# Local and global attention with a gated feed-forward: the global queries of four heads on one tile of 128 partitions

## The chip, the core and the metric

The kernel runs on one core of a Trainium2 chip. The metric is the device time of one execution in microseconds. The kernel before takes 1253.52 us (median of three runs, 1249.87 to 1254.31); its profiled execution took 1242.87 us.

## The reference

There are 8 batches of 8 heads, with 512 local and 32 global positions and 64 channels a head. Each global query sees all 544 keys; each local query sees the 32 global keys and the local ones within 32 positions. The result of all heads, 512 wide, goes through a gated feed-forward with 1536 hidden channels.

```
s_g = scale * q_g @ concat(k_g, k_l).T          # 32 x 544 a head
out_g = softmax(s_g) @ concat(v_g, v_l)
s_l = concat(scale * q_l @ k_g.T, where(|i - j| <= 32, scale * q_l @ k_l.T, -1e9))
out_l = softmax(s_l) @ concat(v_g, v_l)
x = attention output as (8 * 544) x 512
y = (sigmoid(x @ w_gate) * (x @ w_val)) @ w_out
```

## The kernel before

**Precision.** The feed-forward, and the attention of most heads, run on TensorE as fp32r with operands split into a high and a low part (`hi`, and `kl` or `lo`), so that two or three products stand for one in fp32. The first heads run natively in fp32 (tiles with `nat` or `first` in their names): batch 0, and the first four heads of batch 1. What is native has no low part to subtract.

**The feed-forward stream** (`ffn_stream`, L380 to L441) sets the order. Per hidden slice of 128 channels and 512 tokens it multiplies twelve matmuls for the gate (`bank_g`), twelve for the value (`bank_v`, both L395) and twelve for the output (`bank_o`, L430), in blocks of four. After each block the generator yields, a clock `now` moves by one unit (half for 256 tokens), and all attention events that have come due are emitted there. A scheduler then orders each engine's instructions within what is emitted. After the opening, the attention of a batch of 512 tokens is emitted during the 108 units of the feed-forward of the batch before. So between the blocks of four feed-forward matmuls stand short visits of attention work.

**Attention events** (`att_events`, L444). A head has two local units of two blocks of 128 queries each and one global unit, four units of `now` apart. A unit is a generator with four stages, run 0, 3, 6 and 9 units after its start (`STAGES`); in the opening the distances are shorter.

**A local unit** (L232): scores for a window of 224 keys a block (L241); mask and maximum on DVE (L255), exp on ACT (L258); scaling by the sum's reciprocal into `p_buf` (L229); four transposes of 128x128 on TensorE (L272), copied by ACT and subtracted by DVE (L283, L284); products with V (L302, L303); copy, sum and sum of halves on ACT, DVE and GpSimd (L305 to L307). Blocks at the two ends of the sequence use masks of their own that blank 32 of the 224 columns.

**A global unit** (`global_unit`, L309) does the same for the 32 global queries of one head on 32 partitions: scores in two PSUM tiles (L321, L323), two maxima on DVE (L326, L327) and their scaling (L328), two exps on ACT (L330, L331), sum, reciprocal and scaling of the 32x576 row tile `pg_buf` on DVE (L333, L334, L229), five transposes of 32 rows (L339), copy and subtraction (L345, L346), and five products with V (L354). For the first two batches V is the stationary operand and the result comes out transposed (L363) into `xg32`; for the others the 32 queries are the rows of the result, collected in `xgq` and transposed at the end (`split_globals`, L531), before the feed-forward of the 256 global tokens.

**Space.** Eight PSUM banks: four for `bank_o`, four in turn for everything else (tag `att`: gate and value accumulators, scores, transposes, products). A bank is free again when its last reader is done. The split V of a head (`vhl`) has two buffers.

**The opening.** Before and beside the first feed-forward items the kernel converts the weights from their 64-bit layout, mostly on DVE (`convert`, L135 to L155).

Of the kernel before, what the change touches and what calls it, by code (L numbers as in the profile page):

```python
# [56 lines left out]
def kernel(ctx, tc, qk, v, w_gate, w_val, w_out, out_l, out_g):  # L57
# [158 lines left out]
    def split_v(T):  # L216
# [14 lines left out]

    def local_unit(T, blocks, x32s, h, col0):  # L232
# [4 lines left out]
        for i, j in enumerate(blocks):  # L237
            qj = ks[0][:, qcol(j) - q0:qcol(j) - q0 + P]
            for t, (kt, k0) in enumerate(zip(ks, k0s)):
                js = slice(k0 + j * BLK, k0 + j * BLK + WIN)  # L240
                nc.tensor.matmul(s_ps[:, i, 0:WIN], qj, kt[:, js], start=t == 0, stop=t == last)  # L241
# [67 lines left out]
    def global_unit(T, b, h):  # L309
        ks, k0s, q0 = T["qk"], T["k0"], T["q0"]  # L310
        nat = T["native"]
        last = len(ks) - 1
# [13 lines left out]
        nc.vector.tensor_reduce(mg[:, 0:1], saf, axis=AX.X, op=ALU.max)  # L326
        nc.vector.tensor_reduce(mg[:, 1:2], sb, axis=AX.X, op=ALU.max)  # L327
        nc.vector.tensor_scalar(mg[:, 2:3], mg[:, 0:1], mg[:, 1:2], -0.125, op0=ALU.max, op1=ALU.mult)  # L328
# [1 line left out]
        nc.scalar.activation(pg[:, 0:512], saf, AF.Exp, bias=mg[:, 2:3], scale=0.125, accum_out=sg[:, 0:1])  # L330
        nc.scalar.activation(pg[:, 544:576], sb, AF.Exp, bias=mg[:, 2:3], scale=0.125, accum_out=sg[:, 1:2])  # L331
        yield
        nc.vector.tensor_scalar(mg[:, 3:4], sg[:, 0:1], sg[:, 1:2], 1e-9, op0=ALU.add, op1=ALU.add)  # L333
        nc.vector.reciprocal(mg[:, 3:4], mg[:, 3:4])  # L334
        scaled(0, pg[:, 0:576], pg[:, 0:576], mg[:, 3:4])
        yield
        pt_ps = ps.tile([P, 5, 32], F32, name="bank_y", tag="att", bufs=4)
        for j in range(5):
            nc.tensor.transpose(pt_ps[:, j], pg[:, j * P:(j + 1) * P], ident[0:32, 0:32])  # L339
        if nat:  # L340
            pt = att.tile([P, 5, 32], F32, name="ptg_nat", tag="ptg", bufs=1)
            nc.scalar.copy(pt, pt_ps)
        else:
            pt = att.tile([P, 5, 64], F32R, name="ptg", bufs=1)
            nc.scalar.copy(pt[:, :, 0:32], pt_ps)  # L345
            nc.vector.tensor_tensor(pt[:, :, 32:64], pt_ps, pt[:, :, 0:32].bitcast(F32), op=ALU.subtract)  # L346
        yield
        vt = T["v"]
        if b > 1:
            g0 = (b - 2) * SG  # L350
            xg = xgq[g0 // P][g0 % P:g0 % P + SG, h * D:(h + 1) * D]
            o_ps = ps.tile([64, 2 * D], F32, name="bank_x", tag="att", bufs=4)
            for j in range(5):
                nc.tensor.matmul(o_ps, pt[:, j, :], vt[:, (VM + VS)[j], :], start=j == 0, stop=j == 4)  # L354
# [253 lines left out]
```

## Time and profile before

| | |
|---|---|
| timed, median of 3 runs | 1253.52 us |
| profiled execution | 1242.87 us |
| its span, first to last instruction | 1240.0 us |
| TensorE busy | 1210.8 us, 98% |
| VectorE (DVE) busy | 884.1 us, 71% |
| ScalarE (ACT) busy | 780.4 us, 63% |
| GpSimd (POOL) busy | 432.4 us, 35% |
| mean granted TensorE clock | 0.989 |

TensorE's busy time counts the overlap of matmuls in flight once, but each matmul's own duration (about 0.4 us for 512 columns) is longer than its distance to the next one. Distances between starts tell what a matmul costs in the stream. A window's row gives its length, the busy time of each engine with the number of instructions, the granted clock, the share of the DMA engines and GB/s. A group's row ends in busy time, mean duration and the idle time just before it, with what ended that.

### The profile page before, as it was taken

What the parts mean: (1) busy time and instruction counts of PE and PEld (TensorE: products, weight loads), DVE (VectorE), ACT (ScalarE), POOL (GpSimd) and SP (SyncE); (2) the same over time, 40 slices, a digit from 0 to 9 for tenths busy, and PEclk for the clock granted to TensorE, in tenths of its full rate; (3) what the DMA queues carried; (4) which work ended last, traced back from release to release, by engine and by line L of the source; (5) the groups of instructions that cost most, each with busy time, mean ns of one, the idle gap of its engine ahead of it and who ended that gap; (6) DMA issues with size and microseconds to landing.
All of it is one profiled execution on the core that took longest, in us unless ns stands there. A gap on an engine that the chain in (4) does not pass through costs nothing.

```text
span 1240.0 us, 20451 instructions
## 1 busy us (share of the span) xinstructions
PE 1210.8 (98%) x6892; PEld 990.1 (80%) x6892; DVE 884.1 (71%) x2555; ACT 780.4 (63%) x1901; POOL 432.4 (35%) x453
## 2 busy tenths in 40 slices
PE   8899989999999999999999999999999999999998
PEld 6677768887887888888888888887787888888897
DVE  6798976868777777867776877777876777633343
ACT  5677767756666676757765776766675677523233
POOL 2334443524444244434443444424443444100000
PEclk9799989999999999999999999999999999999999
DMA  6677854333333333333333343333333332121243
GB/s 227 216 246 237 271 183 119 105 111 109 91 104 112 121 93 110 110 109 102 112 97 117 118 110 109 93 115 109 98 105 123 102 92 89 51 100 54 69 136 119
DMA packets 59495, 151.88 MB, mean 122 GB/s; under 512 B 6144, under 2 KB 19456, under 8 KB 59392
## 3 DMA queue, kind: packets, MB, share of 16 engines
q1 hardware_dynamic: 59392, 150.59, 39.8%
q8 instruction: 54, 0.88, 0.3%
q14 instruction: 49, 0.40, 0.1%
HBM read 135.36 MB, written 15.20 MB: 121 GB/s over the span
## 4 chain that ended last, share of the span: by engine, by line
PE 82%; DVE 11%; ACT 3%; issue 2%; DMA 1%; POOL 0%; DVEq 0%; ACTq 0%; POOLq 0%
PE bank_v L395 21%; PE bank_g L395 21%; PE bank_o L430 19%; PE bank_x L241 5%; PE bank_y L272 4%; PE bank_y L339 2%; PE bank_x L321 2%; PE bank_x L303 2%; PE bank_x L302 2%; DVE p_buf L229 2%; DVE bank_v L414 1%; DVE bank_v L413 1%; PE bank_x L354 1%; DMA out_dram<-ob 1%; ACT s_sb L258 1%
## 5 line engine op out<-in xcount | busy, mean ns | idle before, releaser
L395 PE MATMUL bank_g<-xt,wg 128*128 128x512 f32 (+1 forms) x1440 | 339.4, 371 | 3.2 <-DVE hh L417 1.5
L430 PE MATMUL bank_o<-wo,hh 128*128 128x512 f32 x1224 | 333.1, 403 | 0.6 <-ACT hh L416 0.3
L395 PE MATMUL bank_v<-xt,wv 128*128 128x512 f32 (+1 forms) x1440 | 332.2, 368 | 0.9 <-DVE mn L408 0.3
L395 PEld LDWEIGHTS bank_g<-xt,wg 128*128 128x128 f32 x1440 | 238.7, 191 | 43.4 <-DVE hh L417 3.8
L395 PEld LDWEIGHTS bank_v<-xt,wv 128*128 128x128 f32 x1440 | 237.6, 190 | 38.9 <-issue 1.3
L430 PEld LDWEIGHTS bank_o<-wo,hh 128*128 128x128 f32 x1224 | 215.4, 189 | 39.5 <-ACT hh L416 2.3
L258 ACT ACTIVATE s_sb<-s_sb,nm 128x224 f32<-128x224 f32 x240 | 113.9, 475 | 103.1 <-DVE nm L255 101.9
L210 POOL TENSOR_TENSOR kl<-qk_raw,qk_hi 128x704 fp32r<-128x704 f32 x52 | 88.6, 1704 | 192.9 <-ACT qk_hi L209 192.9
L229 DVE TENSOR_SCALAR p_buf<-s_sb,r 128x128 f32<-128x128 f32 (+1 forms) x443 | 132.5, 344 | 4.3 <-PE bank_y L272 0.7
L307 POOL TENSOR_TENSOR x<-t 64x256 f32<-64x256 f32 x104 | 78.1, 751 | 150.6 <-DVE t L306 146.7
L403 ACT ACTIVATE th<-bank_g 128x512 f32<-128x512 f32 (+1 forms) x120 | 63.4, 529 | 101.0 <-PE bank_g L395 100.3
L408 DVE TENSOR_SCALAR mn<-bank_g 128x512 f32<-128x512 f32 (+1 forms) x108 | 67.1, 622 | 78.7 <-ACT th L403 77.2
L416 ACT CAST hh<-bank_v 128x512 fp32r<-128x512 f32 (+1 forms) x120 | 62.6, 522 | 86.4 <-DVE bank_v L414 85.6
L413 DVE TENSOR_TENSOR bank_v<-bank_v,mn 128x512 f32<-128x512 f32 (+1 forms) x120 | 73.5, 612 | 46.1 <-PE bank_v L395 37.3
L255 DVE CUSTOM_DVE_ANT_0 s_sb<-bank_x,masks 128x224 f32<-128x224 f32 x240 | 84.3, 383 | 27.9 <-PE bank_x L241 25.8
L272 PE MATMUL bank_y<-ident,p_buf 128*128 128x128 f32 x496 | 78.4, 279 | 9.3 <-DVE p_buf L229 6.9
L209 ACT CAST qk_hi<-qk_raw 128x1248 fp32r<-128x1248 f32 x52 | 64.2, 1234 | 33.0 <-PE bank_y L323 31.8
L272 PEld LDWEIGHTS bank_y<-ident,p_buf 128*128 128x128 f32 x496 | 58.6, 141 | 32.9 <-DVE t L306 8.3
L417 DVE TENSOR_TENSOR hh<-bank_v,hh 128x512 fp32r<-128x512 f32 (+1 forms) x120 | 72.1, 601 | 17.3 <-ACT hh L416 16.8
L212 POOL TENSOR_TENSOR qk_hi<-qk_raw,qk_hi 64x256 fp32r<-64x256 f32 x104 | 81.5, 804 | 4.1
L306 DVE TENSOR_TENSOR t<-bank_x,t 64x512 f32<-64x512 f32 x104 | 70.4, 677 | 10.8 <-ACT t L305 10.3
L284 DVE TENSOR_TENSOR pt<-bank_y,pt 128x512 fp32r<-128x512 f32 x104 | 70.5, 678 | 9.8 <-ACT pt L283 9.7
(120 smaller groups left out, 1925.3 us busy)
## 6 DMA issues: line engine op xcount, KB each, us to landing
wo<-wo_dram SPq DMA_DIRECT2D x116, 512.0 KB, 3.4
qk_raw<-in_qk_dram SPq DMA_DIRECT2D x104, 312.0 KB, 4.4
v_raw<-in_v_dram SPq DMA_DIRECT2D x52, 256.0 KB, 2.6
out_dram<-ob SPq DMA_DIRECT2D x34, 256.0 KB, 2.7
xt<-in_w_gate_dram SPq DMA_DIRECT2D x12, 512.0 KB, 4.6
xt<-in_w_val_dram SPq DMA_DIRECT2D x12, 512.0 KB, 4.0
xt<-in_w_out_dram SPq DMA_DIRECT2D x12, 512.0 KB, 4.4
v_nat<-in_v_dram SPq DMA_DIRECT2D x8, 512.0 KB, 5.2
```

The source lines that it names most:

```text
L210: nc.gpsimd.tensor_tensor(kl, t[:, K0:Q1], hi[:, K0:Q1].bitcast(F32), op=ALU.subtract)
L212: nc.gpsimd.tensor_tensor(hi[64:128, r], t[64:128, r], hi[64:128, r].bitcast(F32), op=ALU.subtract)
L229: nc.vector.tensor_scalar(out, in_, by, None, op0=ALU.mult)
L255: anchor[0] = nc.vector.tensor_tensor_reduce(out=s_sb[:, i], in0=s_ps[:, i, 0:WIN], in1=masks[:, m], scale=-0.125, scalar=3.0e38, op0=ALU. ...
L258: nc.scalar.activation(s_sb[:, i], s_sb[:, i], AF.Exp, bias=nm[:, i:i + 1], scale=-1.0, accum_out=sm[:, i:i + 1])
L272: nc.tensor.transpose(pt_ps[:, 2 * i + t], pb[:, i, t * P:(t + 1) * P], ident)
L284: nc.vector.tensor_tensor(pt[:, 1], pt_ps, pt[:, 0].bitcast(F32), op=ALU.subtract)
L307: nc.gpsimd.tensor_tensor(dst, t0[:, :, 0], t0[:, :, 1], op=ALU.add)
L395: nc.tensor.matmul(acc, w[a][:, t, fs], xt[:, c, t, x0:x0 + ntok], start=n == 0, stop=n == 11)
L413: nc.vector.tensor_tensor(acc, acc, mn, op=ALU.mult)
L417: nc.vector.tensor_tensor(hh[:, 1, 0:ntok], acc, hh[:, 0, 0:ntok].bitcast(F32), op=ALU.subtract)
L430: nc.tensor.matmul(o_ps[t], ph[:, a, t * P:(t + 1) * P], pwo[:, c], start=f2 == 0 and i == 0, stop=f2 == NF - 1 and i == 2)
```

## The change

The global queries of four heads (`GH = 4`) share one tile. `global_unit` becomes two functions. `global_scores` runs for each head at its old place: it multiplies the scores and lets ACT copy them, unscaled, to the head's 32 partitions of `pg`, which now has 128. `global_group` runs once every four heads, right after the fourth head's scores: one maximum, one exp, one scaling for all 128 rows, in one stage; six units later five transposes of 128x128 into two PSUM banks, copy and subtraction; three units later 20 products with V (5 for each head) into one bank, and one copy, one sum and one sum of halves. It always writes the queries as rows to `xgq`, which now has two tiles of 128; `xg32` is gone. For native heads the probabilities become the stationary operand and V the moving one (64 elements in place of 32). V's buffers go from two to five.

Beside that, the first and last blocks of a sequence compute only their 192 columns that count (`span`): scores, maximum, exp and one scaling are narrower, two of the three masks go, and the host's layout of the side tiles of V shifts by 32 rows to fit.

The diff, cut to its core:

```diff
+KALL = SL + SG
+GH = 4
 STAGES = (0, 3, 6, 9)
+GSTAGES = (0, 6, 9)
...
-    pg = const.tile([32, 5 * P], F32, name="pg_buf")
+    pg = const.tile([P, 5 * P], F32, name="pg_buf")
...
-        vhl = spl.tile([P, 8, 2 * D], F32R, name="vhl")
+        vhl = spl.tile([P, 8, 2 * D], F32R, name="vhl", bufs=GH + 1)
...
+    def span(j):
+        return (32 if j == 0 else 0), (WIN - 32 if j == 3 else WIN)
...
+            w0, w1 = span(j)
             for t, (kt, k0) in enumerate(zip(ks, k0s)):
-                js = slice(k0 + j * BLK, k0 + j * BLK + WIN)
-                nc.tensor.matmul(s_ps[:, i, 0:WIN], qj, kt[:, js], start=t == 0, stop=t == last)
+                js = slice(k0 + j * BLK + w0, k0 + j * BLK + w1)
+                nc.tensor.matmul(s_ps[:, i, w0:w1], qj, kt[:, js], start=t == 0, stop=t == last)
...
-    def global_unit(T, b, h):
+    def global_scores(T, row):
...
-        mg = small.tile([32, 4], F32, name="mg")
-        saf = sa.rearrange("p a c -> p (a c)")
-        nc.vector.tensor_reduce(mg[:, 0:1], saf, axis=AX.X, op=ALU.max)
-        nc.vector.tensor_reduce(mg[:, 1:2], sb, axis=AX.X, op=ALU.max)
...
+        rows = slice(SG * row, SG * (row + 1))
+        nc.scalar.copy(pg[rows, 0:SL], sa.rearrange("p a c -> p (a c)"))
+        nc.scalar.copy(pg[rows, SL:KALL], sb)
+
+    def global_group(Ts, b, g):
+        nat = Ts[0]["native"]
+        mg = small.tile([P, 4], F32, name="mg")
+        p = pg[:, 0:KALL]
+        nc.vector.tensor_reduce(mg[:, 0:1], p, axis=AX.X, op=ALU.max)
+        nc.vector.tensor_scalar(mg[:, 1:2], mg[:, 0:1], -0.125, None, op0=ALU.mult)
+        nc.scalar.activation(p, p, AF.Exp, bias=mg[:, 1:2], scale=0.125, accum_out=mg[:, 2:3])
+        nc.vector.tensor_scalar_add(mg[:, 3:4], mg[:, 2:3], 1e-9)
+        nc.vector.reciprocal(mg[:, 3:4], mg[:, 3:4])
+        scaled(0, p, p, mg[:, 3:4])
         yield
+        banks = [ps.tile([P, n, GH, SG], F32, name="bank_y", tag="att", bufs=4) for n in (4, 1)]
+        for j in range(5):
+            o = banks[j // 4][:, j % 4].rearrange("p r q -> p (r q)")
+            nc.tensor.transpose(o, pg[:, j * P:(j + 1) * P], ident)
...
+        o_ps = ps.tile([2 * SG, GH, 2 * D], F32, name="bank_x", tag="att", bufs=4)
+        for r, T in enumerate(Ts):
+            for j in range(5):
+                nc.tensor.matmul(o_ps[:, r], pt[:, j, r].rearrange("p c q -> p (c q)"), T["v"][:, tiles[j], :],
+                                 start=j == 0, stop=j == 4)
+        y = att.tile([SG, GH, 2 * D], F32, name="yq", tag="t0", bufs=1)
...
+                if i == nu:
+                    ev.append((t0, 2, lambda T=T, h=h: global_scores(T, h % GH)))
+                    if h % GH < GH - 1:
+                        continue
+                for o in STAGES if i < nu else GSTAGES:
```

On TensorE, in a steady batch, this is a stretch of the program before (one head's five transposes, L339, and its five products, L354, between feed-forward blocks L395 and L430 and a local unit's scores L241):

```order
L395 MATMUL bank_g<-xt,wg_113 128x512 x4
L339 MATMUL bank_y<-ident,pg_buf 128x32 x5
L395 MATMUL bank_v<-xt,wv_115 128x512 x4
L395 MATMUL bank_v<-xt,wv_116 128x512 x4
L241 MATMUL bank_x<-qk_hi 128x224
L241 MATMUL bank_x<-kl,qk_hi 128x224
L241 MATMUL bank_x<-qk_hi 128x224
L241 MATMUL bank_x<-kl,qk_hi 128x224
L395 MATMUL bank_v<-xt,wv_115 128x512 x4
L354 MATMUL bank_x<-vhl,ptg 64x128 x5
```

Such a pair of visits stands there for every head. In the changed program the stretch behind a fourth head's scores is this (L389 and L424 are the feed-forward, L300 and L301 a local unit's products with V, L339 the group's transposes; after them eight more L424 and then `L360 MATMUL bank_x<-vhl,ptg 64x128 x20`, the group's products):

```order
L389 MATMUL bank_v<-xt,wv_110 128x512 x4
L389 MATMUL bank_v<-xt,wv_111 128x512 x4
L300 MATMUL bank_x<-pt,vhl 128x256
L301 MATMUL bank_x<-pt,vhl 128x256
L300 MATMUL bank_x<-pt,vhl 128x256
L301 MATMUL bank_x<-pt,vhl 128x256
L389 MATMUL bank_v<-xt,wv_110 128x512 x4
L339 MATMUL bank_y<-ident,pg_buf 128x128 x5
L424 MATMUL bank_o_3135<-wo,hh 128x512
L424 MATMUL bank_o_3136<-wo,hh 128x512
L424 MATMUL bank_o_3137<-wo,hh 128x512
L424 MATMUL bank_o_3138<-wo,hh 128x512
```

The five transposes are now as wide as a local unit's, and heads one to three of a group leave only their scores in the row. On DVE, before, one head's softmax (L326 to L229 on `pg_buf`) stands like this ahead of a local unit's sum of products (L306) and subtraction (L284):

```order
L326 TENSOR_REDUCE mg<-bank_x 32x1
L327 TENSOR_REDUCE mg<-bank_y 32x1
L328 TENSOR_SCALAR mg<-mg 32x1
L333 TENSOR_SCALAR mg<-sg 32x1
L334 RECIPROCAL mg<-mg 32x1
L229 TENSOR_SCALAR pg_buf<-pg_buf,mg 32x576
L306 TENSOR_TENSOR t_6335<-bank_x,t_6335 64x512
L284 TENSOR_TENSOR pt<-bank_y,pt 128x512
```

In the changed program DVE has the group's softmax (L329 to L222 on `pg_buf`) and, later, its two subtractions (L345) among the feed-forward's operations (L402 to L411):

```order
L329 TENSOR_REDUCE mg<-pg_buf 128x1
L330 TENSOR_SCALAR mg<-mg 128x1
L332 TENSOR_SCALAR mg<-mg 128x1
L333 RECIPROCAL mg<-mg 128x1
L222 TENSOR_SCALAR pg_buf<-pg_buf,mg 128x544
L304 TENSOR_TENSOR t_4339<-bank_x,t_4339 64x512
L282 TENSOR_TENSOR pt<-bank_y,pt 128x512
L402 TENSOR_SCALAR mn<-bank_g 128x512
L304 TENSOR_TENSOR t_4385<-bank_x,t_4385 64x512
L407 TENSOR_TENSOR bank_v<-bank_v,mn 128x512
L345 TENSOR_TENSOR ptg<-bank_y,ptg 128x16x32
```

The block of softmax operations stands in DVE's row once for four heads; the operation that waits for exp (L332) has the same local operations behind it as L333 before.

More of the change, by code (lines that the diff above doesn't have):

```diff
@@ L193, in load_v @@
             if T["h"] % ng == 0:
-                t = spl.tile([P, ng, nw, D], F32, name="v_nat", tag="vhl")
+                t = spl.tile([P, ng, nw, D], F32, name="v_nat", tag="vhl", bufs=GH + 1)
                 nc.sync.dma_start(t, v[n:n + ng, :, c].rearrange("n p j d -> p n j d"))
@@ new lines, in global_group @@
+    def global_group(Ts, b, g):
[8 more added lines that the diff above has]
+        scaled(0, p, p, mg[:, 3:4])
+        yield
+        banks = [ps.tile([P, n, GH, SG], F32, name="bank_y", tag="att", bufs=4) for n in (4, 1)]
+        for j in range(5):
+            o = banks[j // 4][:, j % 4].rearrange("p r q -> p (r q)")
+            nc.tensor.transpose(o, pg[:, j * P:(j + 1) * P], ident)
+        pt = att.tile([P, 5, GH, 2, SG], F32 if nat else F32R, name="ptg_nat" if nat else "ptg", tag="ptg", bufs=1)
+        for bank, t in zip(banks, (pt[:, 0:4], pt[:, 4:5])):
+            hi, lo = t[:, :, :, 0], t[:, :, :, 1]
+            nc.scalar.copy(hi, bank)
+            if not nat:
+                nc.vector.tensor_tensor(lo, bank, hi.bitcast(F32), op=ALU.subtract)
@@ L336, in global_unit @@
         yield
-        pt_ps = ps.tile([P, 5, 32], F32, name="bank_y", tag="att", bufs=4)
-        for j in range(5):
-            nc.tensor.transpose(pt_ps[:, j], pg[:, j * P:(j + 1) * P], ident[0:32, 0:32])
+        g0 = b * SG
+        xg = xgq[g0 // P][g0 % P:g0 % P + SG, g * GH * D:(g + 1) * GH * D].rearrange("q (r d) -> q r d", d=D)
+        tiles = VM + VS[:1]
         if nat:
[L341 to L354, printed above, removed]
-            y = att.tile([32, 2 * D], F32, name="yq", bufs=1)
-            nc.scalar.copy(y, o_ps[32:64])
-            nc.vector.tensor_tensor(y, o_ps[0:32], y, op=ALU.add)
-            nc.gpsimd.tensor_tensor(xg, y[:, 0:D], y[:, D:], op=ALU.add)
-            return
@@ L360, in global_unit @@
-        xg = xg32[prow:prow + 64, kt, b * SG:(b + 1) * SG]
-        o_ps = ps.tile([64, 32] if nat else [P, 64], F32, name="bank_x", tag="att", bufs=4)
-        for j in range(5):
-            nc.tensor.matmul(o_ps, vt[:, (VM + VS)[j], :], pt[:, j, :], start=j == 0, stop=j == 4)
-        if nat:
+            o_ps = ps.tile([SG, GH, D], F32, name="bank_x", tag="att", bufs=4)
+            for r, T in enumerate(Ts):
+                for j in range(5):
+                    nc.tensor.matmul(o_ps[:, r], pt[:, j, r, 0], T["v"][:, tiles[j], :], start=j == 0, stop=j == 4)
@@ L531, in split_globals @@
     def split_globals():
[L532 to L534 removed]
+        g0 = 0
         for q in xgq:
```

65 lines of the change are left out of this document (25 added, 40 removed).

## The prediction

> **What bounds the kernel now.** I read the page's busy table first, then the windows by stage, then TensorE's timeline inside one batch, then the groups by form and the waits.
>
> ```profile
> span 1240.0 us, 20451 instructions
> PE 1210.8 (98%) x6892; PEld 990.1 (80%) x6892; DVE 884.1 (71%) x2555; ACT 780.4 (63%) x1901; POOL 432.4 (35%) x453
> 56.00:168.50 112.50, 101.94 (x681) 79.99 (x681) 103.60 (x269) 82.25 (x245) 47.05 (x34) 0.97 0.77 249
> 531.00:667.00 136.00, 135.88 (x758) 110.81 (x757) 101.81 (x307) 91.88 (x214) 56.22 (x60) 1.00 0.37 109
> ...
> L152 DVE SCALAR_TENSOR_TENSOR xt<-xt 128x512 uint32<-128x512 uint32 x27 | 24.6, 911 | 0.0
> ```
>
> TensorE is busy 98% of the span. The two windows (columns after the length: PE, PEld, DVE, ACT, POOL busy, granted clock) show two stages. A steady batch, 531 to 667, holds TensorE without a gap; DVE has a quarter of the time free and ACT a third. Six such batches fill 260 to 1075. In the opening, 56 to 168.5, DVE is busy 103.6 of 112.5 us (92%) most of all with converting weights (its costliest group in this window is L152's, the last row), and TensorE stands idle 112.5 - 101.9 = 10.6 us. So in the batches only what TensorE's own stream sheds counts; in the opening DVE work counts too.
>
> Matmul busy times overlap, so I price a visit of attention work between feed-forward matmuls by start times. TensorE's timeline of one head:
>
> ```profile
> 676.32 2.93 PE L430 MATMUL bank_o<-wo,hh 128*128 128x512 f32 x12
> 679.09 1.09 PE L395 MATMUL bank_g<-xt,wg 128*128 128x512 f32 x4
> ...
> 682.33 1.10 PE L395 MATMUL bank_v<-xt,wv 128*128 128x512 f32 x4
> 683.26 0.60 PE L272 MATMUL bank_y<-ident,p_buf 128*128 128x128 f32 x4
> 683.62 2.11 PE L395 MATMUL bank_v<-xt,wv 128*128 128x512 f32 x8
> 685.56 0.28 PE L321 MATMUL bank_x<-qk_hi 128*32 128x256 f32 x1
> ...
> 692.88 1.09 PE L395 MATMUL bank_g<-xt,wg 128*128 128x512 f32 x4
> 693.90 0.49 PE L339 MATMUL bank_y<-ident,pg_buf 32*128 32x32 f32 x5
> 694.32 2.13 PE L395 MATMUL bank_v<-xt,wv 128*128 128x512 f32 x8
> 696.29 0.27 PE L241 MATMUL bank_x<-qk_hi 128*128 128x224 f32 x1
> 696.40 0.27 PE L241 MATMUL bank_x<-kl,qk_hi 128*128 128x224 f32 x1
> ...
> 696.73 1.11 PE L395 MATMUL bank_v<-xt,wv 128*128 128x512 f32 x4
> 697.68 0.46 PE L354 MATMUL bank_x<-vhl,ptg 128*64 128x128 f32 x5
> 697.98 1.13 PE L430 MATMUL bank_o<-wo,hh 128*128 128x512 f32 x4
> 698.95 0.60 PE L272 MATMUL bank_y<-ident,p_buf 128*128 128x128 f32 x4
> ```
>
> Twelve feed-forward matmuls take 679.09 - 676.32 = 2.77 us, 0.231 each. From 692.88 to 696.29 there are twelve of them and the five global transposes: 3.41 - 2.77 = **0.64 us** for the visit. From 682.33 to 685.56, twelve and four full 128x128 transposes: 3.23 - 2.77 = 0.46, or 0.115 each. From 696.73 to 698.95, eight and the five global products with V: 2.22 - 1.85 = **0.37**; within it they follow each other at 0.30 / 5 = 0.06, so 0.07 is the price of the visit itself.
>
> **The change part by part.** *Global transposes.* Five per group of four heads replace twenty. They now have the shape of the local ones, so 5 x 0.115 = 0.58 us. A batch has eight heads, two groups: 8 x 0.64 - 2 x 0.58 = 3.96 us less.
>
> [...]
>
> *Products with V.* Twenty in one visit, same shape: 20 x 0.06 + 0.07 = 1.27 us in place of 4 x 0.37 = 1.48; two groups, 0.42 us less. Six batches: 6 x (3.96 + 0.42) = **26.3 us**.
>
> The other 16 heads stand in the opening: batch 0, native fp32, and batch 1, whose first four heads are native too. Their four groups: the group of split heads saves 4 x 0.64 - 0.58 + 0.42 / 2 = 2.2 us. The three native groups save 3 x (4 x 0.64 - 0.58) = 5.9 on transposes. Their products with V swap operands:
>
> ```profile
> 57.76 1.05 PE L321 MATMUL bank_x<-qk_nat 64*32 64x256 f32 x4
> 58.65 0.22 PE L323 MATMUL bank_y<-qk_nat 64*32 64x32 f32 x2
> ...
> 59.47 0.77 PE L363 MATMUL bank_x<-ptg_nat,v_nat 128*64 128x32 f32 x10
> 60.16 0.74 PE L395 MATMUL bank_v<-xt,wv 128*128 128x256 f32 x4
> ```
>
> Before, ten instructions (two per fp32 product) take 0.69 us a head, 0.069 each. After, 64 elements move instead of 32. A 256-element native one takes 0.89 / 4 = 0.22, so 64 take 0.055 if time goes by length: between 0.055 and 0.11 (twice 0.055) each, -1.7 to +4.9 us over the 120 instructions. I take 0, nearest to the row 0.069. **8.1 us** in all for this stage's TensorE work.
>
> *Softmax.* These are the DVE and ACT operations of one global head now:
>
> ```profile
> L326 DVE TENSOR_REDUCE mg<-bank_x 32x1 f32<-32x512 f32 x64 | 43.1, 673 | 10.9 <-PE bank_y L323 8.2 <-PE bank_x L321 2.6
> L327 DVE TENSOR_REDUCE mg<-bank_y 32x1 f32<-32x32 f32 x64 | 10.9, 170 | 0.0
> L328 DVE TENSOR_SCALAR mg<-mg 32x1 f32<-32x1 f32 x64 | 12.8, 200 | 1.9
> L333 DVE TENSOR_SCALAR mg<-sg 32x1 f32<-32x1 f32 x64 | 12.8, 200 | 48.6 <-ACT pg_buf L331 47.5
> L334 DVE RECIPROCAL mg<-mg 32x1 f32<-32x1 f32 x64 | 9.5, 149 | 1.4
> L229 DVE TENSOR_SCALAR pg_buf<-pg_buf,mg 32x576 f32<-32x576 f32 x64 | 46.1, 720 | 1.5
> L330 ACT ACTIVATE pg_buf<-bank_x,mg 32x512 f32<-32x512 f32 x64 | 43.1, 673 | 10.7 <-DVE mg L328 10.5
> L331 ACT ACTIVATE pg_buf<-bank_y,mg 32x32 f32<-32x32 f32 x64 | 16.8, 262 | 0.0
> L305 ACT COPY t<-bank_x 64x512 f32<-64x512 f32 x104 | 60.6, 583 | 12.3 <-PE bank_x L303 10.3
> ```
>
> On DVE a head costs 0.673 + 0.170 + 0.200 + 0.200 + 0.149 + 0.720 = 2.11 us; a 512-wide operation takes 0.673 on 32 partitions (L326) and 0.678 on 128 (L284, below), so a whole group costs about 0.72 + 0.2 + 0.2 + 0.15 + 0.68 = 1.95 where four heads cost 8.4. ACT gets two copies a head, 0.583 + 0.26, and one exp a group where it had two exps a head, so it is lighter too. In the batches TensorE's stream hides all this: DVE had 34 us free in 136. In the opening it does not. About nine heads lie in 56 to 168.5; 9 x 2.11 = 19 us of DVE become about 4. DVE's load falls from 103.6 to some 88 in 112.5, and the 10.6 us that TensorE waits there, plus the clock that it loses after them, can shrink. Bounds: 0, if the waits are chains and not load, and 10.6. I take **6 us**, nearer to the upper row, since the waits I can see are for DVE:
>
> ```profile
> 113.67 0.47 PE L339 MATMUL bank_y<-ident,pg_buf 32*128 32x32 f32 x5 [1.94 <-DVE pg_buf L229]
> ...
> 168.52 0.63 PE L272 MATMUL bank_y<-ident,p_buf 128*128 128x128 f32 x4 [3.63 <-DVE p_buf L229]
> ```
>
> *The chain of a group.* Copies 0.583 + 0.262, maximum 0.72, scale 0.2, exp about 0.71, sum and reciprocal 0.35, scaling 0.68: 3.5 us without queues. On TensorE, between the fourth head's scores and the group's transposes, stand 24 feed-forward matmuls and three local visits: 24 x 0.231 + 0.46 for transposes + 2 x 0.46 for products (four matmuls of half the width each, so four halves of 0.231) = 6.9 us. The margin of 3.4 us covers ACT's and DVE's queues. Behind the transposes stand twelve matmuls, 2.8 us, and in them the ACT copies and DVE subtractions of two banks:
>
> ```profile
> L345 ACT CAST ptg<-bank_y 128x160 fp32r<-128x160 f32 x52 | 15.1, 291 | 11.3 <-PE bank_y L339 10.8
> L284 DVE TENSOR_TENSOR pt<-bank_y,pt 128x512 fp32r<-128x512 f32 x104 | 70.5, 678 | 9.8 <-ACT pt L283 9.7
> DVE mg L333 <- ACT pg_buf L331: 47.5, 38, 1.8
> PEld bank_y L272 <- DVE t L306: 8.3, 18, 0.6
> ```
>
> A 512-wide copy is 0.58, the subtraction 0.68 and the small one about 0.3: 1.6 us against 2.8, where one head's 160-wide pair had cost 0.6 (L345 0.29 and as much on DVE). Feed-forward work on DVE stands in between (0.68 each), so the twenty products may wait: 0 to 0.7 us (one such operation), I take 0.2 for 12 groups in the batches, **-2.4 us**. In DVE's row the maximum, the wait for exp and the scaling stand in one block, and behind it the local unit's addition that frees a bank. That is not new: DVE waited 38 times for exp, 1.25 us each, now 16 times at most.
>
> *Edges.* The first and last blocks multiply 192 columns, not 224. A 224-column matmul follows the one before at 0.11 us (696.29 to 696.40); by length 192 take 0.016 less, over 208 of them 3.3 us; at a fixed price 0. Four 128-column transposes also took 0.115 apart, so I take the fixed price nearly whole: **0.5 us**. Shorter exps and maxima lie on DVE and ACT under cover. The mask copies and memsets at the start stand beside the first loads: nothing. The last global tile of 128 rows in place of 64, and four small splits less, stand under 2.8 us of feed-forward matmuls as before: nothing; about 0.3 us if not.
>
> **Sum.** 26.3 + 8.1 + 6 - 2.4 + 0.5 = 38.5 us. Against the profiled execution of 1242.87 us (span 1240.0 and 2.87 around it) that is 1204.4. The three timed runs have a median of 1253.52, 10.65 above the profiled one; I take the same microseconds off it: **1215 us**.
>
> **The rivals.**
>
> *A, the opening gives nothing.* DVE's remaining conversions keep TensorE waiting as long, and waits at 20 products rise to 0.7 us for 12 groups. The windows speak for it (92% of DVE, most of it weights). Then 26.3 + 8.1 + 0.5 - 8.4 = 26.5: 1227 us.
>
> *B, the banks.* Attention and feed-forward share four PSUM banks. A group's transposes take two at once for copy and subtraction, and the products a third for 0.58 + 0.68. If the feed-forward accumulators wait for them, every group loses the 1.6 us above: 16 x 1.6 = 26 us, and 1241 us remains. For it: L272 waited 18 times for the addition that frees a bank. Against: each wait was under 0.6, and the heads hold their score banks for a copy instead of a maximum and an exp.
>
> *C, slower: the group comes late.* If the chain, with what is queued on ACT and DVE, is longer than its 6.9 us (less in the opening, where mostly half-width matmuls stand between), TensorE idles at the transposes, and then the clock drops:
>
> ```profile
> 114.90:118.20 3.30, 3.30 (x19) 3.24 (x19) 2.09 (x5) 1.49 (x3) 1.76 (x1) 0.50 0.61 136
> ```
>
> After the idle 1.94 us before 113.67 the granted clock is 0.50 for 3.3 us, which costs another 1.7. A group that is 2 us late would lose 3.7, sixteen of them 59: 1215 + 59 = 1274 us. It ends slower from 38.5 / 16 = 2.4 us per group on, that is a delay of about 0.7 us and the dropped clock, each time. Against: in the batches the margin is 3.4 us, and the granted clock of 531 to 667 is 1.00.
>
> [...]
>
> *D, it saves nothing on TensorE:* the transposes' time was other work's shadow. The start times exclude it in the batches.
>
> **How the numbers follow.** Forecast 0.70, A 0.17, B 0.06, C 0.06, D 0.01. The range: below, all 10.6 us of the opening, the 1.7 us of the swapped products, the 3.3 us of full edge price and no waits at the products make 38.5 + 4.6 + 1.7 + 2.8 + 2.4 = 50.0 us, 1203.5, rounded to 1203. Above, A with the swapped products at 4.9 us dearer, 1232, and a little of B: 1236. B still ends over 0.5% faster (the three runs spread 4.4 us, 0.35%; 0.5% is about what can be told from no change). Faster 0.92, same 0.03, slower 0.05.
>
> **What would show it.** In the profile after: 80 group transposes at about 0.58 us a visit and 20 products at 1.27; a steady batch 4.3 us shorter, about 131.2 us; DVE under 0.9 of its time in 56 to 168 and fewer idle microseconds of TensorE there. Wrong if TensorE waits at the group's transposes or products for DVE in the batches, if the accumulators wait for ptg's subtraction, or if half-clock windows follow the group visits.

## The result and the profile after

The changed kernel takes 1262.68 us (median of four runs, 1260.87 to 1263.75) against 1253.61 for the kernel before in the same runs: a ratio of 1.0077, 95% interval 1.0053 to 1.0101. The prediction was 1215 us, so it had the wrong sign. The profiled execution of the kernel before was faster than its timed runs here (1242.87 us, not 1253.61), so between the two profiles the loss is larger, 19.1 us of span (1240.0 to 1259.1).

The profiled execution took 1260.87 us. Its page begins like this, and the window row below it is a steady batch, a section of 432 feed-forward matmuls (length, then PE, PEld, DVE, ACT, POOL busy, granted clock, DMA share, GB/s):

```profile
span 1259.1 us, 19319 instructions
...
PE 1182.2 (94%) x6652; PEld 986.0 (78%) x6652; DVE 782.3 (62%) x2186; ACT 754.8 (60%) x1719; POOL 414.9 (33%) x408
...
509.90:652.50 142.60, 133.29 (x723) 110.98 (x722) 88.87 (x259) 88.84 (x193) 54.48 (x54) 0.98 0.36 103
```

TensorE has 240 instructions less and 28.6 us less busy time than before (1210.8). Yet its idle time, span minus busy, is 1259.1 - 1182.2 = 76.9 us; before it was 29.2. DVE and ACT are both lighter. So the saving is there and something new makes TensorE wait, in the steady batches: this one takes 142.6 us and not 135.6. The same section of the kernel before:

```profile
515.70:651.30 135.60, 135.49 (x753) 110.46 (x752) 101.45 (x307) 91.91 (x215) 56.23 (x60) 1.00 0.37 109
```

The changed kernel's waits say for what (engine, tile and line, what it waited for: total us, times, longest):

```profile
PE bank_y L319 <- DMA out_dram<-ob: 22.9, 4, 6.2
PE bank_y L319 <- DVE mn L402: 6.3, 2, 6.0
PE bank_v L389 <- DVE pt L282: 9.7, 12, 2.7
PE bank_x L300 <- DVE pt L282: 9.1, 8, 1.7
ACT vhl L214 <- DMA v_raw<-in_v_dram: 84.8, 36, 4.1
POOL vhl L215 <- ACT vhl L214: 103.3, 43, 3.7
SPq L193 <- POOL vhl L215: 121.5, 48, 7.0
SPq L193 <- DMA v_raw<-in_v_dram: 77.8, 31, 5.2
```

None of TensorE's large waits is at the group's transposes or products. The new row is ACT's: 84.8 us at L214, the cast of a head's V into its high part, waiting for the load of that V. Before, the same cast had none; its group's row in that kernel ends in the idle time ahead of it:

```profile
L221 ACT CAST vhl<-v_raw 128x512 fp32r<-128x512 f32 x52 | 31.9, 614 | 0.0
```

Five times, once in a batch, TensorE stands some 6 us at L319, the small score matmul. One of those places on TensorE, DVE, ACT and SP (start, duration, what, and in brackets the idle time ahead with its releaser):

```profile
686.66 0.28 PE L317 MATMUL bank_x<-kl,qk_hi 128*32 128x256 f32 x1
692.49 0.23 PE L319 MATMUL bank_y<-qk_hi 128*32 128x32 f32 x1 [5.54 <-DMA out_dram<-ob]
...
689.92 0.69 DVE L432 TENSOR_SCALAR ob<-bank_o 128x512 f32<-128x512 f32 x1 [5.46 <-DMA out_dram<-ob]
...
691.74 0.69 DVE L402 TENSOR_SCALAR mn<-bank_g 128x512 f32<-128x512 f32 x1 [0.85 <-ACT th L397]
...
679.72 0.62 ACT L214 CAST vhl<-v_raw 128x512 fp32r<-128x512 f32 x1 [1.97 <-DMA v_raw<-in_v_dram]
680.25 0.58 ACT L410 CAST hh<-bank_v 128x512 fp32r<-128x512 f32 x1
...
684.29 0.62 ACT L214 CAST vhl<-v_raw 128x512 fp32r<-128x512 f32 x1 [2.55 <-DMA v_raw<-in_v_dram]
...
672.54 14.10 SPq L193 DMA_DIRECT2D v_raw<-in_v_dram  x4
686.73 0.86 SPq L433 DMA_DIRECT2D out_dram<-ob  x2
```

Read it from the bottom. SP's queue has four V loads in a row. V as loaded has one buffer, so each load waits until the head before has been cast (0.62 us) and subtracted (1.29 us, the median on GpSimd): the last two casts start 4.57 us apart, and the four loads hold the queue for 14.10 us. Two output stores stand behind them and go out at 686.73. Until they land, DVE's copy into `ob` (L432) waits, and L402, the last reader of a gate accumulator, stands behind it on DVE; TensorE's L319 needs that bank. Meanwhile ACT has stood 1.97 and 2.55 us at casts with feed-forward work queued behind.

The two windows of that place show what follows:

```profile
686.70:692.50 5.80, 0.26 (x4) 0.01 (x1) 1.69 (x5) 1.84 (x4) 0.00 (x0) 0.94 0.88 281
692.50:698.00 5.50, 5.50 (x19) 4.62 (x20) 3.90 (x9) 3.71 (x7) 2.80 (x3) 0.50 0.11 40
```

After 5.8 us with hardly any matmul the granted clock is 0.50 for 5.5 us more.

Where do the bunches come from? ACT's row in the scheduled order has three casts of V in nine rows, where before one stands every twenty or so:

```
L214 CAST vhl<-v_raw 128x8x64
L397 ACTIVATE th<-bank_g 128x512
L404 ACTIVATE th<-th 128x512
L403 ACTIVATE mn<-mn 128x512
L214 CAST vhl<-v_raw 128x8x64
L410 CAST hh<-bank_v 128x512
L255 ACTIVATE s_sb,sm<-s_sb,nm 128x192
L255 ACTIVATE s_sb,sm<-s_sb,nm 128x224
L214 CAST vhl<-v_raw 128x8x64
```

With V for a cast of V and Q for one of queries and keys, a batch reads `VVVVQQQQVVQVVQQQ` now and `QVQVQVQVQVQVQVQV` before.

### The profile page after: what moved, and what is told of

It is laid out like the page before. It is cut to its first block, busy times and chain, and to the rows that moved or that the text cites. A ratio compares the mean times of both kernels' runs of the same rounds, so it can differ in the third digit from the quotient of the medians.

```text
span 1259.1 us, 19319 instructions
## 1 busy us (share of the span) xinstructions
PE 1182.2 (94%) x6652; PEld 986.0 (78%) x6652; DVE 782.3 (62%) x2186; ACT 754.8 (60%) x1719; POOL 414.9 (33%) x408
## 4 chain that ended last, share of the span: by engine, by line
PE 66%; DVE 11%; ACT 8%; DMA 7%; POOL 4%; issue 4%; SPq 0%; POOLq 0%; DVEq 0%; ACTq 0%
PE bank_o L424 18%; PE bank_v L389 17%; PE bank_g L389 16%; DMA v_raw<-in_v_dram 5%; PE bank_x L238 4%; PE bank_y L270 3%; POOL vhl L215 3%; ACT s_sb L255 3%; DMA out_dram<-ob 2%; DVE p_buf L222 2%; PE bank_x L300 2%; PE bank_x L301 2%; PE bank_x L317 1%; DVE xt L144 1%; DVE s_sb L252 1%
## 5 line engine op out<-in xcount | busy, mean ns | idle before, releaser
L389 PE MATMUL bank_v<-xt,wv 128*128 128x512 f32 (+1 forms) x1440 | 332.5, 368 | 9.7 <-DVE pt L282 9.7
L424 PE MATMUL bank_o<-wo,hh 128*128 128x512 f32 x1224 | 337.6, 408 | 3.0 <-DVE hh L411 2.0
L389 PE MATMUL bank_g<-xt,wg 128*128 128x512 f32 (+1 forms) x1440 | 333.8, 367 | 0.9 <-POOL xt L372 0.5
L389 PEld LDWEIGHTS bank_v<-xt,wv 128*128 128x128 f32 x1440 | 240.6, 192 | 46.6 <-issue 9.3
L389 PEld LDWEIGHTS bank_g<-xt,wg 128*128 128x128 f32 x1440 | 239.1, 191 | 38.7 <-issue 2.1
L424 PEld LDWEIGHTS bank_o<-wo,hh 128*128 128x128 f32 x1224 | 222.6, 194 | 44.5 <-DVE hh L411 2.8
L255 ACT ACTIVATE s_sb<-s_sb,nm 128x192 f32<-128x192 f32 (+1 forms) x240 | 110.6, 462 | 91.8 <-DVE nm L252 91.5
L222 DVE TENSOR_SCALAR p_buf<-s_sb,r 128x128 f32<-128x128 f32 (+2 forms) x443 | 116.7, 301 | 8.0 <-PE bank_y L270 2.4
L402 DVE TENSOR_SCALAR mn<-bank_g 128x512 f32<-128x512 f32 (+1 forms) x108 | 67.5, 625 | 84.1 <-ACT th L397 83.2
L411 DVE TENSOR_TENSOR hh<-bank_v,hh 128x512 fp32r<-128x512 f32 (+1 forms) x120 | 72.9, 608 | 60.7 <-ACT hh L410 60.7
L252 DVE CUSTOM_DVE_ANT_0 s_sb<-bank_x,masks 128x192 f32<-128x192 f32 (+1 forms) x240 | 80.6, 369 | 34.4 <-PE bank_x L238 25.8
L215 POOL TENSOR_TENSOR vhl<-v_raw,vhl 128x512 fp32r<-128x512 f32 x52 | 67.3, 1294 | 104.0 <-ACT vhl L214 103.3
L270 PEld LDWEIGHTS bank_y<-ident,p_buf 128*128 128x128 f32 x496 | 62.5, 144 | 28.8 <-DVE p_buf L222 6.7
L214 ACT CAST vhl<-v_raw 128x512 fp32r<-128x512 f32 x52 | 32.1, 618 | 87.1 <-DMA v_raw<-in_v_dram 84.8
```

The costliest lines, as they stand in the source:

```text
L215: nc.gpsimd.tensor_tensor(vhl[:, :, D:2 * D], t, vhl[:, :, 0:D].bitcast(F32), op=ALU.subtract)
L222: nc.vector.tensor_scalar(out, in_, by, None, op0=ALU.mult)
L252: anchor[0] = nc.vector.tensor_tensor_reduce(out=s_sb[:, i, w], in0=s_ps[:, i, w], in1=mid[:, w], scale=-0.125, scalar=3.0e38, op0=ALU.add ...
L255: nc.scalar.activation(s_sb[:, i, w], s_sb[:, i, w], AF.Exp, bias=nm[:, i:i + 1], scale=-1.0, accum_out=sm[:, i:i + 1])
L270: nc.tensor.transpose(pt_ps[:, 2 * i + t], pb[:, i, t * P:(t + 1) * P], ident)
L389: nc.tensor.matmul(acc, w[a][:, t, fs], xt[:, c, t, x0:x0 + ntok], start=n == 0, stop=n == 11)
```

## The experiments

Each run is compared with runs of the kernel before on the same chip (medians of these 1243.2 us for the first four kernels, 1250.6 for the next four, 1242.2 for the four after and 1249.8 for the last), so its ratio counts more than its microseconds. Theories of the first four runs: **Q** (queue): the 20 products release V of four heads at once, the schedule then puts V's loads and casts in bunches, and engines and queues stand at them. **N**: the number of V buffers alone does it. **G**: the group's own visits, banks and DVE block cost the time.

### Buffers alone, paced loads, paced casts, stores elsewhere

*`before_v5`*, the kernel before with V's buffers at five:

```diff
-        vhl = spl.tile([P, 8, 2 * D], F32R, name="vhl")
+        vhl = spl.tile([P, 8, 2 * D], F32R, name="vhl", bufs=5)
```

> The kernel before with one edit: V's split buffers go from two to five, as in the change. Theory Q (queue): the stalls come from V's buffers that fall free four at a time after the twenty products, so that V loads stand in bunches on the DMA queue; five buffers that fall free one at a time do nothing, ratio to before 0.995 to 1.005. Rival N (number): the five buffers alone let the scheduler place V casts and loads too early, ratio 1.01 to 1.03. Rival G (group): the group's own visits, banks and DVE block cost the time; nothing here, 0.995 to 1.005.

Measured: 1244.23 us, ratio to the kernel before 1.0009 (0.9964 to 1.0055). N is out; the order still has one V load a head.

*`load_paced`*, the changed kernel with each V load queued on SP behind the last output-weight load or output store (`sp_last`):

```diff
-        nc.sync.dma_start(t[:, c], v[n][:, c])
+        with tc.issue_after(sp_last[0].ins):
+            nc.sync.dma_start(t[:, c], v[n][:, c])
```

> The changed kernel with each V load queued behind the last wo load or output store that the program emitted before it, so no V load stands ahead of an older store. Theory Q: the waits of about 6 us at the small score product (L319), once a batch, go with the half clock after them, 6 x (5.7 + 1.7) = 44 us; about 1218 us, 1212 to 1232. Rival G: the waits stay, 1255 to 1265. Rival N: partly, 1240 to 1255, since ACT still has its casts ahead of the loads.

Measured: 1229.54 us, ratio 0.9874 (0.9806 to 0.9942), inside Q's range. The 6 us waits at L319 are gone, but not all of the loss (lines are two higher here):

```profile
PE bank_g L391 <- DVE pt L284: 20.1, 10, 4.5
...
ACT vhl L216 <- DMA v_raw<-in_v_dram: 43.9, 15, 5.9
```

ACT still stands 43.9 us at casts, and TensorE waits 20.1 us for the subtraction that follows ACT's copy of `pt`. The edit moves the casts too: ACT's row reads `QVQVQVQVQVQVQQVV` a batch here, so this run alone doesn't tell SP's queue from ACT's.

*`cast_paced`*, the changed kernel with each V cast queued on ACT behind the last emitted exp of a local unit (`act_last`):

```diff
-        nc.scalar.copy(vhl[:, :, 0:D], t)
+        with tc.issue_after(act_last[0].ins):
+            nc.scalar.copy(vhl[:, :, 0:D], t)
```

> The changed kernel with each V cast on ACT queued behind the last local exp that the program emitted before it. Theory Q: ACT no longer waits for V loads (84.8 us before this edit, under 10 after), the single raw V buffer is released late and evenly, so the loads spread out as well; both the 6 us waits and the 1.7 us waits of local products go: about 1215 us, 1208 to 1228. Rival G: 1255 to 1265.

Measured: **1202.51 us, ratio 0.966 (0.9596 to 0.9723)**. The order has one V load and one cast a head again. The page, a steady batch, the cast's group row (busy, mean ns | idle ahead) and TensorE's largest waits:

```profile
PE 1162.4 (97%) x6652; PEld 974.6 (81%) x6652; DVE 809.8 (67%) x2186; ACT 753.3 (63%) x1719; POOL 415.6 (35%) x408
...
493.90:626.40 132.50, 130.51 (x724) 109.73 (x723) 93.06 (x259) 88.80 (x193) 54.76 (x54) 1.00 0.39 111
...
L216 ACT CAST vhl<-v_raw 128x512 fp32r<-128x512 f32 x52 | 31.5, 606 | 0.0
...
PE bank_v L391 <- DVE pt L284: 11.8, 12, 1.0
PE bank_x L302 <- DVE pt L284: 4.8, 6, 1.3
```

The cast waits for nothing. The same 6652 TensorE instructions take 19.8 us less busy time than in the changed kernel (mean granted clock 0.991 in place of 0.975), and idle falls from 76.9 to 1201.9 - 1162.4 = 39.5 us. So the grouped queries do bring about what they should. The last two rows, 16.6 us, are the large new ones among TensorE's waits (the kernel before has 0.2 us at that subtraction); they are what is left for G.

*`store_act`*, the changed kernel with the output stores on ACT's queue:

```diff
-                            nc.sync.dma_start(C2["dst"][t * P:(t + 1) * P, :], ob)
+                            nc.scalar.dma_start(C2["dst"][t * P:(t + 1) * P, :], ob)
```

> The changed kernel with the output stores issued from ACT's queue in place of SP's; V loads stay in bunches. Theory Q: the stores no longer stand behind V loads, the 6 us waits go, the 1.7 us waits of local products for ACT (17 us in all) stay: about 1225 us, 1218 to 1238. Rival G: 1255 to 1265. If the bunched loads hurt by other ways than the stores (wo loads behind them), also 1245 to 1260.

Measured: 1258.35 us, ratio 1.0097 (1.0061 to 1.0133), far above Q's 1218 to 1238. The 6 us wait splits in two, of up to 2.9 us at L317 and 2.3 at L319, and ACT's wait at casts stays (86.9 us, 36 times). This doesn't tell SP from ACT, since ACT's own stores stand behind its blocked casts: two go out at 684.64, right behind the cast at 683.50 that had waited 2.53 us.

### Is it holding V, or the group?

**O** is Q made sharper: V freed in fours leads the schedule to place casts in ACT's row ahead of loads that have not landed.

*`before_hold`*, the kernel before with five V buffers and, at each fourth head, four one-element products that keep all four in use till then:

```diff
+        held.append(vt)
+        if h % 4 == 3:
+            for i, u in enumerate(held):
+                nc.vector.tensor_tensor(keep[:, i:i + 1], u[0:1, 0, 0:1].bitcast(F32),
+                                        pt[0:1, 0, 0:1].bitcast(F32), op=ALU.mult)
+            held.clear()
```

> The kernel before with five V buffers, and at each fourth head four tiny DVE products (one element of each of the four heads' V by one of the fourth head's transposed probabilities) that keep all four V buffers in use till then; the tiny products' own results go nowhere. In the scheduled order the V loads and casts then stand in the same bunches as in the changed kernel (VVVV QQQQ VV Q VV QQQ a batch), with the old global units. Theory O (order: V freed in fours bunches the casts ahead of their loads): the stall of ACT and its 6 us of TensorE per batch appear here too, some 30 to 60 us: 1275 to 1300 us, ACT waiting 60 us or more for V loads. Theory G (the group's own visits, banks and DVE block cost the time): nothing here, 1241 to 1248 us.

Measured: 1282.8 us, ratio 1.0289 (1.0223 to 1.0354). Its waits and a steady batch (lines about ten higher than before):

```profile
PE bank_g L402 <- DVE hh L424: 14.7, 7, 2.5
PE bank_y L325 <- DVE mn L415: 10.8, 6, 2.3
...
ACT vhl L223 <- DMA v_raw<-in_v_dram: 58.4, 27, 5.2
...
530.00:671.30 141.30, 137.12 (x753) 111.89 (x753) 104.18 (x315) 91.68 (x215) 56.17 (x60) 0.99 0.36 103
```

Without any grouped query, holding V for four heads gives the old kernel the same order of casts, waits at them (58.4 us, where 60 or more were expected) and a batch of 141.3 us in place of 135.6. That shows O, and speaks against G.

*`store_pool`*, as `store_act` but on GpSimd's queue (`nc.gpsimd.dma_start`).

> The changed kernel with the output stores issued from GpSimd's queue, which waits for neither V loads nor ACT's stores. If stores that stand behind V loads on SP's queue cost the 6 us per batch, they go here (about 36 us, with the half clock behind them up to 45): 1218 to 1230 us. If it is ACT, standing at casts whose loads have not landed, TensorE waits elsewhere instead: 1250 to 1262 us, with ACT's wait for V loads still at 80 us or more.

Measured: 1268.21 us, ratio 1.0168 (1.009 to 1.0246), outside both ranges. GpSimd's row at the same place:

```profile
688.73 1.29 POOL L215 TENSOR_TENSOR vhl<-v_raw,vhl 128x512 fp32r<-128x512 f32 x1 [3.43 <-ACT vhl L214]
689.96 1.10 POOL L433 DMA_DIRECT2D out_dram<-ob  x2
```

The stores stand behind GpSimd's subtraction of V, and that waits for ACT's cast. V's chain of load, cast and subtraction runs through SP, ACT and GpSimd, and in each of the three runs the queue that takes the stores is held up by it: by 14.10 us of V loads on SP in the changed kernel, 2.53 us at a cast on ACT, 3.43 us at a subtraction on GpSimd. So these two runs with moved stores don't tell whether the stores' place or the blocked casts count.

*`both_paced`*: both edits above, paced loads and paced casts.

> The changed kernel with both the V casts queued behind the last emitted local exp on ACT and the V loads behind the last output-weight load or store on SP. If ACT's blocked casts are all of it: the same as with paced casts alone, 1200 to 1206 us. If loads that stand ahead of weights or stores still cost something there: 1190 to 1198 us. Theory G: no lower than 1202 us, and TensorE's waits for DVE's subtraction in the feed-forward stay at 12 to 17 us.

Measured: 1205.03 us, ratio 0.9659 (0.9595 to 0.9722), the same as with paced casts; ACT's waits for V loads are 5.1 us, so the loads cost nothing more. This run and `load_paced` pace the loads alike, and ACT's row reads `QVQVQVQVQVQVQQVV` a batch in both; they differ in how late the casts stand in it. With ACT's waits for V loads 38.8 us shorter (43.9 to 5.1) the span is 18.9 us shorter (1223.2 to 1204.3). So ACT's blocked casts cost time by themselves; how much of the rest SP's late stores cost stays open.

*`cast_split`*: paced casts, and the group's softmax in two stages:

```diff
         nc.scalar.activation(p, p, AF.Exp, bias=mg[:, 1:2], scale=0.125, accum_out=mg[:, 2:3])
+        yield
```

with `GSTAGES = (0, 3, 6, 9)`.

> The changed kernel with paced V casts, and the group's softmax cut in two stages: sum, reciprocal and scaling are emitted three units after the exp, transposes three units later than before. Theory G (what is left of waits, some 17 us at the feed-forward's accumulators behind DVE's subtraction, is DVE standing in the group's block for the exp): these waits halve, 1192 to 1198 us. If they come from the local units' own chains (ACT copy, then DVE): no change, 1200 to 1206 us.

Measured: 1204.96 us, ratio 0.9658 (0.9595 to 0.9722); the waits stay at 11.8 and 4.9 us. G's last part falls: the block around the group's exp is not what these waits are for.

### Controls, the bunch's size, the edges, and what is left

*`before_hold_paced`*: `before_hold` with paced casts.

> The kernel before with V held till the fourth head (as in the run that held it) and, beside that, each V cast queued on ACT behind the last emitted local exp; the scheduled order has one V load and one cast per head again. Theory O: the whole loss of holding goes and pacing gives nothing beyond it, 1241 to 1247 us, a steady batch at 135 to 137 us, ACT's wait for V loads under 5 us. If pacing casts is a gain of its own, which the paced changed kernel would then owe to it and not to the grouped queries: 1200 to 1225 us.

Measured: 1248.53 us, a little above the 1241 to 1247 expected, ratio 1.0023 (0.9987 to 1.0059). The loss of holding goes, and pacing brings nothing beyond that: the gain of `cast_paced` over the kernel before is the change's own.

*`before_hold2`*: V held for pairs, with three buffers (`if h % 2 == 1`).

> The kernel before with three V buffers, V held till every second head; its casts stand in pairs. Theory O, if the loss goes with the number of casts in a bunch that come ahead of their loads (one raw buffer: every cast after the first waits for a whole load): one wait in two heads in place of three in four, a third to two thirds of the 40 us that the hold of four cost, 1255 to 1268 us. If a pair is hidden by slack: 1241 to 1247 us.

Measured: 1287.0 us, ratio 1.0342 (1.0288 to 1.0397): as much as for fours. That the loss goes with the number of casts in a bunch is wrong; ACT waits less (42.6 us, 22 times) and TensorE loses the same. Whether two casts in a row are enough by themselves was then open.

*`hold2_raw2`*: the same pairs, with two buffers for V as loaded:

```diff
-        t = raw.tile([P, 8, D], F32, name="v_raw")
+        t = raw.tile([P, 8, D], F32, name="v_raw", bufs=2)
```

> The kernel before with V held till every second head and three split buffers, as in the run that held pairs, and two buffers for V as loaded in place of one; the casts stand in the same pairs in ACT's order, but the second load of a pair no longer waits for the first head's cast and subtraction. If the casts cost time because they come ahead of loads that the single raw buffer holds back: ACT's 42.6 us of waits for V loads fall under 10 and most of the 45 us goes, 1240 to 1255 us. If two casts in a row cost it by themselves (ACT's 1.2 us ahead of the local units, or GpSimd's two subtractions), it stays at 1275 to 1290 us.

Measured: 1250.16 us, ratio 1.0038 (1.0005 to 1.0072). The casts stand in the same pairs; a steady batch:

```profile
521.50:657.40 135.90, 135.52 (x754) 110.80 (x752) 103.79 (x314) 92.07 (x215) 56.15 (x60) 1.00 0.37 108
```

ACT no longer waits for a V load, and nearly all of the loss is gone. So it is not casts in a row that cost, but a cast placed ahead of a load that the one raw buffer holds back. This cure was not tried on the changed kernel.

*`before_span`*: the narrower edges alone on the kernel before.

```diff
+                w0, w1 = span(j)
+                js = slice(k0 + j * BLK + w0, k0 + j * BLK + w1)
+                nc.tensor.matmul(s_ps[:, i, w0:w1], qj, kt[:, js], start=t == 0, stop=t == last)
```

> The kernel before with the narrower edges alone: first and last blocks of a sequence multiply, mask and exponentiate 192 columns. 208 score matmuls. At a fixed price per matmul nothing, at the price by length 3.3 us in all, or 0.4 us a steady batch (135.6 to 135.2): 1237 to 1243 us either way, told apart by the batch's length in the trace.

Measured: 1246.9 us, ratio 1.0025 (1.0003 to 1.0048). No gain; its five steady batches together are 3.6 us longer than before's (685.3 to 681.7). Why stays open.

*`cast_norm`*: paced casts, and every fourth scaling of split heads on ACT (`NORM[0] = "vvvs"`). This tries what is left of the waits: in `cast_paced` four scalings of 1.68 us in all stand on DVE right ahead of the subtraction that TensorE waits for:

```profile
602.35 1.68 DVE L224 TENSOR_SCALAR p_buf<-s_sb,r 128x128 f32<-128x128 f32 x4
603.95 0.68 DVE L284 TENSOR_TENSOR pt<-bank_y,pt 128x512 fp32r<-128x512 f32 x1
```

> The changed kernel with paced V casts, and every fourth scaling of split heads (128x64 or 128x96, or a group's 128x544) on ACT in place of DVE. If what is left of TensorE's waits behind DVE's subtraction (about 17 us) is the four scalings that stand ahead of it on DVE: half of it goes, 1190 to 1197 us. If ACT then becomes late in its turn: 1202 to 1215 us.

Measured: 1200.45 us, ratio 0.9639 (0.959 to 0.9688). The two waits fall from 11.8 to 9.9 and 4.8 to 2.4 us, a quarter and not half, and the time lies between the two ranges; the interval overlaps that of `cast_paced`, so it is level with it. Both beat the kernel before by over 3%.

## Why the prediction was wrong

**The step that failed** is the part "The change part by part". It priced every operation of the group, but not the change's line on V's buffers, and the release of V in fours that stands behind it. No term and no rival speaks of V's loads, casts or of SP's queue: they stood at nothing without a reason, and cost 56.2 us. The times, from sections of 432 feed-forward matmuls counted back from the last one in the trace, in us:

| | up to batch 2 | batch 2 | the next five | the rest | last start |
|---|---|---|---|---|---|
| before | 250.5 | 128.7 | 681.8 | 174.6 | 1235.5 |
| changed | 237.6 | 130.1 | 713.3 | 172.6 | 1253.7 |
| `cast_paced` | 236.3 | 125.1 | 664.3 | 171.8 | 1197.5 |
| `before_hold` | 255.3 | 132.1 | 714.3 | 174.0 | 1275.8 |
| `before_hold2` | 256.3 | 135.9 | 714.7 | 174.0 | 1280.9 |
| `hold2_raw2` | 255.0 | 130.3 | 683.3 | 175.0 | 1243.4 |

The change without its stall is worth 38.0 us (1235.5 to 1197.5), where 38.5 were forecast; the stall takes back 56.2 (1253.7 - 1197.5). That the 38 came out is in part luck, as the terms below show. In the old kernel the same hold costs 40.3, so the two don't simply add. Of the 57 us of span between the changed kernel and `cast_paced`, 37.4 are idle and 19.8 are the slower clock (0.975 against 0.991). Each microsecond that ACT stood for V cost 0.7 us in the changed kernel (57/84.8) and in `before_hold` (40.2/58.4), but 1.1 in `before_hold2` (45.3/42.6); what sets that ratio is not settled.

In the changed kernel's trace the feed-forward is held up behind V. ACT stood 1.97 us at the cast that started at 679.72; `hh`, right behind it in ACT's row, started at 680.25, though DVE's operation that it reads (L408) had ended at 679.22.

**Visits.** Right. In `cast_paced`, where no stall blurs them (L341 are the transposes, L362 the products):

```profile
639.71 1.09 PE L391 MATMUL bank_v<-xt,wv 128*128 128x512 f32 x4
640.64 0.71 PE L341 MATMUL bank_y<-ident,pg_buf 128*128 128x128 f32 x5
641.10 3.03 PE L426 MATMUL bank_o<-wo,hh 128*128 128x512 f32 x12
643.97 1.24 PE L362 MATMUL bank_x<-vhl,ptg 128*64 128x128 f32 x18
...
583.53 1.10 PE L391 MATMUL bank_v<-xt,wv 128*128 128x512 f32 x4
584.47 1.36 PE L362 MATMUL bank_x<-vhl,ptg 128*64 128x128 f32 x20
585.66 0.91 PE L426 MATMUL bank_o<-wo,hh 128*128 128x512 f32 x3
586.41 0.60 PE L272 MATMUL bank_y<-ident,p_buf 128*128 128x128 f32 x4
```

Sixteen feed-forward matmuls at 0.231 and five transposes lie between 639.71 and 643.97: 4.26 - 3.70 = 0.56 us against 0.58. Seven and twenty products lie between 583.53 and 586.41: 2.88 - 1.62 = 1.26 against 1.27.

**Batches.** Six of them lose 3.6 + 17.5 = 21.1 us in `cast_paced`; forecast 26.3 - 2.4 = 23.9. Two misses nearly cancel. The six sections before:

```profile
250.50:1061.00 810.50, 806.88 (x4483) 657.44 (x4481) 609.48 (x1814) 543.69 (x1272) 328.06 (x351) 1.00 0.36 106
```

and in `cast_paced`:

```profile
236.30:1025.80 789.50, 776.04 (x4313) 652.88 (x4312) 550.53 (x1530) 523.75 (x1143) 320.17 (x317) 1.00 0.38 109
```

TensorE's idle time (length minus busy) grows from 3.6 to 13.5 us, where 2.4 were allowed. Its busy time falls by 30.8, where 26.3 were forecast; what gave the other 4.5 is not shown. The rest of the stream gives 2.8 us (174.6 to 171.8) that no term had.

**Opening.** The total is right by luck, 14.2 us against 8.1 + 6 = 14.1. 4.3 us of it lie before the first feed-forward matmul, which starts at 43.3 before and at 39.0 in `cast_paced`. From there to batch 2, before:

```profile
43.30:250.50 207.20, 195.02 (x1303) 159.10 (x1303) 172.75 (x499) 150.31 (x438) 87.12 (x73) 0.95 0.61 196
```

and in `cast_paced`:

```profile
39.00:236.30 197.30, 182.62 (x1227) 149.66 (x1227) 157.61 (x417) 143.39 (x393) 82.06 (x69) 0.96 0.64 198
```

TensorE's busy time falls by 12.4 us, where 8.1 were forecast, and its idle time does not fall: 12.2 us before, 14.7 after. The changed kernel in the window that the prediction used shows the same:

```profile
56.00:168.50 112.50, 101.72 (x649) 79.16 (x647) 95.07 (x230) 81.61 (x225) 44.64 (x34) 0.95 0.74 234
```

DVE falls from 103.6 to 95.1 us, where some 88 were forecast, and TensorE's idle time stays (112.5 - 101.7 = 10.8 us). So the 6 us put down to DVE's relief did not come that way.

**Edges.** Forecast 0.5 us; alone they gained nothing.

**Rivals.** C had the sign and the half clock, but not the place: the group's transposes waited 1.5 us in the whole run. B's place, accumulators behind a subtraction, is where 11.8 of the last 16.6 us are (the other 4.8 are local products that wait for `pt`), yet it is the local units' subtraction (L284) and not the group's. A's premise, that TensorE waits as long in the opening, held, but not its sum: the opening gave 14.2 us where A counts 8.1.

## What to carry to other kernels

When a change lets go of several buffers at once, look at who refills them: follow the loads and casts of that tile in each queue's order, and ask whether a cast can stand there ahead of a load that has not landed. In the changed kernel the raw tile's one buffer made such loads late by a whole turn of load, cast and subtraction (the last two of four casts started 4.57 us apart), and ACT waited 84.8 us for V's loads. In the kernel before with V held, a second raw buffer (ratio 1.0038) or a cast pinned behind work of its own time (1.0023) took the loss away. Engines that looked idle enough, and a sum of operations that came out right, didn't show this here; the order of the queues did.

## What the hardware showed that was not expected

After many gaps of 2 us and longer the granted clock was 0.50. In the changed kernel's trace, between 200 and 1100 us, none of 13 gaps of 0.9 to 1.9 us between starts of matmuls was followed by a granted clock of 0.50; all seven from 2.05 us up were. In `before_hold2` six of twelve gaps of 2.5 to 2.7 us were.

In these traces the outcome went with where the gap fell. In their clock records the changes of the granted clock lie whole steps of 3.41 us apart. In the changed kernel, between 200 and 1100 us, the half clock lasted one step twice (3.41 us) and two steps five times (6.83 us). Two gaps of `before_hold2` in these steps, one of 2.50 us from 779.13 (first two rows, half in each step) and one of 2.65 us from 887.61 (last two):

```profile
777.10:780.50 3.40, 2.22 (x14) 1.69 (x12) 1.58 (x6) 0.84 (x2) 0.44 (x2) 1.00 0.29 77
780.50:783.90 3.40, 2.26 (x12) 1.90 (x12) 2.39 (x6) 2.53 (x4) 2.49 (x2) 1.00 0.36 112
...
886.30:889.70 3.40, 1.49 (x11) 1.09 (x9) 1.04 (x5) 1.52 (x3) 1.16 (x2) 1.00 0.61 231
889.70:893.10 3.40, 2.85 (x7) 2.30 (x8) 1.89 (x5) 3.37 (x8) 1.77 (x2) 0.50 0.28 77
```

The first gap leaves TensorE idle for 1.2 and 1.1 us of its two steps, and the clock stays; the second leaves it idle for 1.9 us of one step, and the next step has half the clock. Counted in the traces of all fifteen kernels, between 200 and 1100 us, there are 3902 steps at full clock. All 34 with TensorE idle for over 1.92 us were followed by half the clock, none of 3857 with less than 1.65 was, and of the 11 between 5 were. So a little over half of a step idle (more than 1.92 of 3.41 us) was always enough here. The gap of 2.65 us was followed by half the clock, an estimated 1.7 us lost in each step of it (half of 3.41), and the one of 2.50 us by nothing.
